# Output stores cut per batch entry, the last copy and its stores moved to other engines, the last gate cut in halves

## The chip, the cores and the metric

The kernel runs on one core of one Trainium2 chip. The metric is device time in microseconds (us) of one execution; the kernel before takes 823.6 us, the median of 3 runs (823.19 to 827.01). The core has a matrix engine (TensorE, PE in the rows; PEld is its weight load), three engines for elementwise work (VectorE or DVE, ScalarE or ACT, GpSimd or POOL), and a fifth, SyncE or SP, which here only issues DMA transfers. Each engine works through its own list of instructions in order and waits on semaphores for the others. A letter q behind a name (SPq) means the engine's sequencer, which issues transfers. The transfers of all of them are carried out by 16 DMA engines.

## The reference

A recurrence over 768 time steps, for 4 batch entries with 8 heads of 40, feeds a gated feed-forward layer:

```python
for t in range(S):                                   # S = 768
    y[:, :, t] = einsum('bhd,bhde->bhe', r_t, state)
    Sa = einsum('bhde,bhe->bhd', state, a_t)
    state = state * w_t[:, :, None, :] - Sa x b_t + v_t x k_t
x = y as (4 * 768, 320)                              # rows: batch entry, then time
h = x @ w_in                                         # 320 -> 2048
g = where(h >= 1, h, where(h <= -1, 0, (h + 1)**2 / 4))
out = g @ w_out                                      # 2048 -> 320, float32
```

## The kernel before

The recurrence runs in 24 chunks of 32 steps, each in two halves of 16 (batch, head) pairs. Lines 139 to 590 load and scale its rows, write them to scratch in DRAM (`scr`), read them back in another order (`ti`, `cg`, `tiab`), and do the chunk's small matrix products. Each 64 steps of finished rows make one of 12 groups: `relayout` (L605 to L614) moves the group's rows from `Y` into `X`, one of two buffers used in turn, with 6 transfers.

The feed-forward layer is the generator `moe`. A group holds 64 steps of 4 batch entries, 256 columns. For each of 8 expert pairs `k` (256 columns of the 2048 each):

- `first` (L631): 16 products of 256 columns into a PSUM bank `ph`, 8 for each half `j` of the pair; the two banks are used in turn.
- `gate`: Relu (L639) and Square (L640) on ScalarE, then minimum and maximum on VectorE (L642), each over the tile of 128 x 512, both halves at once.
- `split`: ScalarE rounds the result to `gh` (L648), GpSimd forms the rest `gl` (L649). Both tiles have one buffer.
- `second` (L661): 12 products of 320 columns with `gh` (8) and `gl` (4) into two PSUM banks `po`. Block 0 of the output (`po[0]`) holds batch entries 0 and 1 of the group's 64 steps, block 1 (`po[1]`) entries 2 and 3.

The loop is staggered: `first` of a pair stands ahead of `second` of the pair before it, and the gate of the new pair runs beside that. After the last pair's `first` and the `second` of the pair before, nothing is left to lay beside the last gate, split and `second`.

At a group's end ScalarE copies the two blocks to `ob` (L664). The stores go into a list, `deferred`; SP issues them (L666) at the next call of `catch_up`, in SP's list among the loads of the recurrence. So for each group SP issues 2 stores of 160 KB, each 128 partitions of `ob` to 2 x 64 rows of 1,280 bytes in `out`: the DRAM side is 2 batch entries, each a run of 64 rows.

The order of all this is written by hand: `feed` pulls so many columns of `moe` into each stage of the recurrence, `fill` and `background` put the preparation of later rows in between. When the recurrence is done, the rest of `moe` is emptied in one loop. `DMAHW0` to `DMAHW7` are 8 semaphores that the transfers of SP (and of ScalarE) use in turn; a transfer waits until the one 8 places ahead has landed.

Of the kernel before, what the change touches and what calls it, by code (L numbers as in the profile page):

```python
# [9 lines left out]
F32 = mybir.dt.float32  # L10
# [5 lines left out]
AF = mybir.ActivationFunctionType  # L16
ALU = mybir.AluOpType
# [3 lines left out]
NB, NHD, D, L = 4, 8, 40, 32  # L21
# [34 lines left out]
def rwkv_moe_kernel(ctx: ExitStack, tc: tile.TileContext, r, k, v, w, a, b, w_in, w_out, ident_d, mask_d, out):  # L56
    nc = tc.nc
# [5 lines left out]
    NF = FF // 128  # L63
# [6 lines left out]
    phs = [psa.tile([128, 512], F32, name=f"ph{i}") for i in range(2)]  # L70
    pos = [psa.tile([128, 512], F32, name=f"po{i}")[:, 0:320] for i in range(2)]
# [4 lines left out]
    half_c = const.tile([128, 1], F32, name="half_c")  # L76
# [6 lines left out]
    mp = ctx.enter_context(tc.tile_pool(name="mp", bufs=1))  # L83
# [13 lines left out]
    Y, Xt = [], {}  # L97
# [46 lines left out]
    flat = lambda x: x.rearrange("p a e -> p (a e)")  # L144
# [449 lines left out]
    groups = [(t, 64) for t in range(0, S, 64)]  # L594
# [23 lines left out]
    ov = out.rearrange("(b s) e -> b s e", b=NB)  # L618
    Xs = {}
    deferred = []  # L620

    def moe():

        def first(g, k):
            t0, nt = groups[g]
            n = NB * nt
            for j in range(2):
                f = 2 * k + j
                fs = slice(128 * (f % 4), 128 * (f % 4) + 128)
                for i, (xi, wi) in enumerate(MM1):  # L630
                    nc.tensor.matmul(  # L631
                        phs[k % 2][:, n * j : n * j + n], lhsT=wt[0, f // 4, wi // 2][:, wi % 2, fs], rhs=Xs[g][:, xi, :], start=i == 0, stop=i == 7
                    )
                    yield 15 * n // 16

        def gate(k):
            ph = phs[k % 2]
            gt = mp.tile([128, 512], F32, tag="gt", name="gt", bufs=2)
            nc.scalar.activation(gt, ph, AF.Relu, bias=half_c, scale=0.5)  # L639
            nc.scalar.activation(gt, gt, AF.Square)  # L640
            yield gt
            nc.vector.scalar_tensor_tensor(out=gt, in0=gt, scalar=1.0, in1=ph, op0=ALU.min, op1=ALU.max)  # L642
            yield

        def split(gt):
            gh = mp.tile([128, 512], F32R, tag="gh", name="gh", bufs=1)
            gl = mp.tile([128, 512], F32R, tag="gl", name="gl", bufs=1)
            nc.scalar.copy(gh, gt)  # L648
            nc.gpsimd.tensor_sub(gl, gt, gh.bitcast(F32))  # L649
            return gh, gl  # L650

        def second(g, k, gt, gh, gl):
            t0, nt = groups[g]
            n = NB * nt
            passes = [(x, i, j) for x, i in ((gh, 0), (gh, 1), (gl, 0)) for j in range(2)]
            for q, (x, i, j) in enumerate(passes):
                w = wt[1, 2 * k + j, 0][:, i, :]
                for i in range(n // 128):
                    ts_ = slice(n * j + 128 * i, n * j + 128 * i + 128)
                    end = q == 5 and k == NF // 2 - 1  # L660
                    nc.tensor.matmul(pos[i], lhsT=x[:, ts_], rhs=w, start=q == 0 and k == 0, stop=end)  # L661
                    if end:
                        ob = mp.tile([128, 320], F32, tag="ob", name="ob", bufs=2)
                        nc.scalar.copy(ob, pos[i])  # L664
                        m = 128 // nt
                        deferred.append(lambda ob=ob, i=i, m=m: nc.sync.dma_start(ov[m * i : m * i + m, t0 : t0 + nt, :], ob))  # L666
                    yield 320

        late = None
        for g in range(len(groups)):  # L670
            while g not in Xs:
                yield None
            for k in range(NF // 2):
                while g == 0 and converted[0] < needs(2 * k + 1):
                    next(wgen)
                if late:
                    late += split(late[2])
                yield from first(g, k)
                parts = gate(k)
                for i, d in enumerate(second(*late) if late else (320,) * 12):  # L680
                    yield d
                    if i == 3:
                        new = (g, k, next(parts))
                    elif i == 8:
                        next(parts)
                late = new
        yield from second(*late, *split(late[2]))

    jobs = []
    for j in range(4):  # L690
# [154 lines left out]
    i = 0  # L845
# [6 lines left out]
    adopt(0)  # L852
    Y.append(y_tile(F32R))
    mgen = moe()
    owed, idle = [0], [True]
    now = [0]
# [120 lines left out]
```

## Time and profile before

| | us |
|---|---|
| median of 3 runs (lowest, highest) | 823.6 (823.19, 827.01) |
| the profiled execution, its own time | 821.57 |
| its span, first to last instruction | 819.8 |
| TensorE busy | 679.4 |
| VectorE busy | 588.8 |
| ScalarE busy | 479.8 |
| GpSimd busy | 457.3 |

The span is what the trace shows; the profiled execution's own time is 1.77 us longer, and this execution lies 2.03 us below the median of the runs. The trace has the start and length of each instruction, what ended each wait, the share of the 16 DMA engines that were busy in any stretch, and the granted clock of TensorE there.

### The profile page before, as it was taken

What the parts mean: (1) busy time and instruction counts of PE and PEld (TensorE: products, weight loads), DVE (VectorE), ACT (ScalarE), POOL (GpSimd) and SP (SyncE); (2) the same over time, 40 slices, a digit from 0 to 9 for tenths busy, and PEclk for the clock granted to TensorE, in tenths of its full rate; (3) what the DMA queues carried; (4) which work ended last, traced back from release to release, by engine and by line L of the source; (5) the groups of instructions that cost most, each with busy time, mean ns of one, the idle gap of its engine ahead of it and who ended that gap; (6) DMA issues with size and microseconds to landing.
All of it is one profiled execution on the core that took longest, in us unless ns stands there. A gap on an engine that the chain in (4) does not pass through costs nothing.

```text
span 819.8 us, 35420 instructions
## 1 busy us (share of the span) xinstructions
PE 679.4 (83%) x15360; PEld 623.2 (76%) x15360; DVE 588.8 (72%) x1327; ACT 479.8 (59%) x1014; POOL 457.3 (56%) x630
## 2 busy tenths in 40 slices
PE   4265445598888688789988899999999999999994
PEld 4254445488777687679977789988899999999993
DVE  7996878778667567886767887767877777775220
ACT  5456666576564455656655566565665666665552
POOL 1305999965235869656648767554466742222331
PEclk9675556778899899999989999999999999999997
DMA  8888985756946636676436664352433324330100
GB/s 300 217 137 222 217 173 150 197 132 151 203 131 154 170 79 162 146 178 150 95 71 154 152 175 102 89 111 39 102 76 79 83 44 100 77 84 19 37 18 16
DMA packets 178714, 102.33 MB, mean 125 GB/s; under 512 B 123976, under 2 KB 171272, under 8 KB 178560
## 3 DMA queue, kind: packets, MB, share of 16 engines
q1 hardware_dynamic: 172288, 78.45, 42.5%
q0 software_dynamic: 6272, 21.63, 9.5%
q8 instruction: 121, 1.98, 1.0%
q14 instruction: 33, 0.27, 0.1%
HBM read 70.88 MB, written 27.53 MB: 120 GB/s over the span
## 4 chain that ended last, share of the span: by engine, by line
PE 49%; POOL 8%; DVE 5%; DMA 4%; ACT 3%; issue 2%; SPq 0%; ACTq 0%; POOLq 0%; DVEq 0%
PE po L661 16%; PE ph L631 16%; PE p L556 5%; PE p L545 3%; PE p L519 3%; DMA scr<-arena 2%; PE p L585 2%; POOL gl L649 2%; PE p L485 2%; POOL lw L369 2%; PE p L529 2%; POOL lw L363 2%; ACT gh L648 1%; DMA cg<-scr 1%; PE p L336 1%
## 5 line engine op out<-in xcount | busy, mean ns | idle before, releaser
L649 POOL TENSOR_TENSOR gl<-gt,gh 128x512 fp32r<-128x512 f32 x96 | 124.3, 1295 | 193.1 <-ACT gh L648 188.5
L631 PE MATMUL ph<-X,w 120*128 120x256 f32 x1536 | 217.3, 294 | 3.9 <-DMA X<-Y 3.6
L631 PEld LDWEIGHTS ph<-X,w 120*128 120x128 f32 x1536 | 196.0, 196 | 11.6 <-issue 4.8
L661 PE MATMUL po<-w,gh 128*128 128x320 f32 x768 | 135.9, 319 | 16.8 <-ACT gh L648 16.7
L661 PEld LDWEIGHTS po<-w,gh 128*128 128x128 f32 x768 | 117.1, 193 | 20.6 <-ACT gh L648 19.8
L642 DVE SCALAR_TENSOR_TENSOR gt<-gt,ph 128x512 f32<-128x512 f32 x96 | 65.8, 686 | 89.3 <-ACT gt L640 75.6
L639 ACT ACTIVATE gt<-ph,half_c 128x512 f32<-128x512 f32 x96 | 66.0, 687 | 54.7 <-PE ph L631 54.5
L563 DVE SCALAR_TENSOR_TENSOR cg<-p,pr 40x160 f32<-40x160 f32 x184 | 59.2, 322 | 53.1 <-PE p L556 51.1
L661 PE MATMUL po<-w,gl 128*128 128x320 f32 x384 | 78.0, 327 | 22.8 <-POOL gl L649 22.8
L369 POOL TENSOR_TENSOR lw<-lw 128x31 f32<-128x31 f32 (+15 forms) x155 | 88.2, 569 | 8.7
L363 POOL TENSOR_TENSOR lw<-lw 128x31 f32<-128x31 f32 (+15 forms) x155 | 85.8, 554 | 9.3
L661 PEld LDWEIGHTS po<-w,gl 128*128 128x128 f32 x384 | 63.0, 198 | 27.1 <-POOL gl L649 27.0
L497 DVE TENSOR_TENSOR cg<-p,mask 32x256 f32<-32x256 f32 x192 | 80.6, 420 | 3.5
L540 ACT ACTIVATE cg<-p 32x160 f32<-32x160 f32 x192 | 56.6, 295 | 26.8 <-PE p L529 12.0
L536 DVE SCALAR_TENSOR_TENSOR cg<-p,mask 32x128 f32<-32x128 f32 x192 | 55.2, 288 | 19.8 <-ACT cg L540 14.5
L550 ACT COPY ss<-p 40x320 f32<-40x320 f32 x92 | 38.6, 419 | 48.7 <-PE p L545 47.1
L556 PE MATMUL p<-cg 128*64 128x72 f32 (+1 forms) x1536 | 66.2, 246 | 0.0
L648 ACT CAST gh<-gt 128x512 fp32r<-128x512 f32 x96 | 59.7, 621 | 10.5 <-DVE gt L642 9.5
L640 ACT ACTIVATE gt<-gt 128x512 f32<-128x512 f32 x96 | 60.7, 632 | 3.1
L545 PE MATMUL p<-cg 128*40 128x40 f32 x1472 | 44.4, 224 | 21.8 <-ACT cg L540 15.4
L545 PEld LDWEIGHTS p<-cg 128*40 128x40 f32 x1472 | 38.1, 136 | 31.5 <-ACT cg L540 22.5
L556 PEld LDWEIGHTS p<-cg 128*64 128x64 f32 x1536 | 60.6, 155 | 0.4 <-issue 0.4
(100 smaller groups left out, 1100.0 us busy)
## 6 DMA issues: line engine op xcount, KB each, us to landing
ti<-scr SPq DMA_DIRECT2D x96, 200.0 KB
scr<-arena POOLq DMA_DIRECT2D x16, 640.0 KB, 5.8
cg<-scr SPq DMA_DIRECT2D x96, 80.0 KB
X<-Y SPq DMA_DIRECT2D x36, 160.0 KB
scr<-wide SPq DMA_DIRECT2D x8, 640.0 KB
w<-in_moe_w_out_dram POOLq DMA_DIRECT2D x16, 320.0 KB, 4.3
tiab<-scr SPq DMA_DIRECT2D x28, 160.0 KB
cg<-scr SPq DMA_DIRECT2D x96, 40.0 KB
```

The lines of the kernel that those rows point to most:

```text
L363: eng.tensor_mul(t3, W3[:, 0:n, j : j + 1].broadcast_to([128, n, m]), L3[:, j + 1 :, j].unsqueeze(1).broadcast_to([128, n, m]),)
L369: eng.tensor_sub(W3[:, 0:n, j + 1 :], W3[:, 0:n, j + 1 :], t3)
L497: nc.vector.tensor_tensor(out=cg[q, f::2, C_X : C_X + 64][:, 4 * i : 4 * i + 4].rearrange("p h (j x) -> p h j x", x=32), in0=ps[quarter(f, ...
L545: nc.tensor.matmul(pst[er[h % 2], h // 2, :], lhsT=cg[:, h, C_S : C_S + D], rhs=cg[:, h, C_G : C_G + D], start=True, stop=True)
L556: nc.tensor.matmul(psv[h // 8][64 * f : 64 * f + 64, h // 2 % 4, 0:n3], lhsT=cgw[:, h * CW + C_G : h * CW + C_G + 64], rhs=cg[:, h, C_R : ...
L631: nc.tensor.matmul(phs[k % 2][:, n * j : n * j + n], lhsT=wt[0, f // 4, wi // 2][:, wi % 2, fs], rhs=Xs[g][:, xi, :], start=i == 0, stop=i ...
L639: nc.scalar.activation(gt, ph, AF.Relu, bias=half_c, scale=0.5)
L640: nc.scalar.activation(gt, gt, AF.Square)
L642: nc.vector.scalar_tensor_tensor(out=gt, in0=gt, scalar=1.0, in1=ph, op0=ALU.min, op1=ALU.max)
L648: nc.scalar.copy(gh, gt)
L649: nc.gpsimd.tensor_sub(gl, gt, gh.bitcast(F32))
L661: nc.tensor.matmul(pos[i], lhsT=x[:, ts_], rhs=w, start=q == 0 and k == 0, stop=end)
```

## The change

- A new helper, `store`, issues one transfer for each batch entry: 64 partitions of `ob` to 64 consecutive rows of `out`, 80 KB. Each group has 4 stores where it had 2.
- Block 1 of the last group is copied by VectorE instead of ScalarE, and its 2 stores are issued by ScalarE. All other stores stay with SP.
- The last pair's gate is a function of its own, `last_gate`. It works on the halves `j` of 256 columns, in the order of the code below, and puts `gh` and `gl` in the buffer of `X` that the last group doesn't use. `second` of the pair ahead of it stands before it in the program. The last `second` takes both `gh` products of half 0 first, then those of half 1.

```diff
+    def store(ob, i, t0, nt, queue):
+        m = 128 // nt
+        for q in range(m):
+            queue.dma_start(ov[m * i + q, t0 : t0 + nt, :], ob[nt * q : nt * q + nt])
...
             passes = [(x, i, j) for x, i in ((gh, 0), (gh, 1), (gl, 0)) for j in range(2)]
+            if (g, k) == at_last:
+                passes = [(gh, i, j) for j in range(2) for i in range(2)] + passes[4:]
...
                         ob = mp.tile([128, 320], F32, tag="ob", name="ob", bufs=2)
-                        nc.scalar.copy(ob, pos[i])
-                        m = 128 // nt
-                        deferred.append(lambda ob=ob, i=i, m=m: nc.sync.dma_start(ov[m * i : m * i + m, t0 : t0 + nt, :], ob))
+                        at_end = g == len(groups) - 1 and i
+                        (nc.vector.tensor_copy if at_end else nc.scalar.copy)(ob, pos[i])
+                        deferred.append(lambda ob=ob, i=i, q=nc.scalar if at_end else nc.sync: store(ob, i, t0, nt, q))
...
+        def last_gate(k):
+            n = NB * groups[-1][1]
+            gt = mp.tile([128, 512], F32, tag="gt", name="gt", bufs=2)
+            spare = flat(Xt[len(groups) % 2])
+            gh, gl = (spare[:, 512 * i : 512 * i + 512] for i in range(2))
+            cols = [slice(n * j, n * j + n) for j in range(2)]
+            for x in cols:
+                nc.scalar.activation(gt[:, x], phs[k % 2][:, x], AF.Relu, bias=half_c, scale=0.5)
+                nc.scalar.activation(gt[:, x], gt[:, x], AF.Square)
+            for x in cols:
+                nc.vector.scalar_tensor_tensor(
+                    out=gt[:, x], in0=gt[:, x], scalar=1.0, in1=phs[k % 2][:, x], op0=ALU.min, op1=ALU.max
+                )
+            for x in cols:
+                nc.scalar.copy(gh[:, x], gt[:, x])
+                nc.gpsimd.tensor_sub(gl[:, x], gt[:, x], gh[:, x].bitcast(F32))
+            return gt, gh, gl
...
                 yield from first(g, k)
+                if (g, k) == at_last:
+                    yield from second(*late)
+                    late = g, k, *last_gate(k)
+                    break
                 parts = gate(k)
...
-        yield from second(*late, *split(late[2]))
+        yield from second(*late)
```

ScalarE's list at the end of the program, before, from the rounding of the pair ahead of the last (`ph_64` is the bank of the last pair, `po_65` and `po_66` are blocks 0 and 1; each row says on which semaphores the instruction waits):

```order
L648 CAST gh<-gt 128x512 [waits DVE_49,PE_49,Pool_49]
L639 ACTIVATE gt<-ph_64,half_c 128x512 [waits PE_49]
L640 ACTIVATE gt<-gt 128x512 [waits Activation_49]
L648 CAST gh<-gt 128x512 [waits DVE_49,PE_49,Pool_49]
L664 COPY ob<-po_65 128x320 [waits DMAHW6_49,PE_49]
L664 COPY ob<-po_66 128x320 [waits DMAHW7_49,PE_49]
```

The same piece of the changed program (`X_1896` is the spare buffer of `X`, where `gh` and `gl` now are):

```order
L654 CAST gh<-gt 128x512 [waits DVE_49,PE_49,Pool_49]
L685 ACTIVATE gt<-ph_64,half_c 128x256 [waits PE_49]
L686 ACTIVATE gt<-gt 128x256 [waits Activation_49]
L685 ACTIVATE gt<-ph_64,half_c 128x256
L686 ACTIVATE gt<-gt 128x256 [waits Activation_49]
L692 CAST X_1896<-gt 128x256 [waits DVE_49] x2
L673 COPY ob<-po_65 128x320 [waits DMAHW3_49,DMAHW2_49,PE_49]
L626 DMA out_dram<-ob 64x320 [waits DMAHW7_49,DVE_49]
L626 DMA out_dram<-ob 64x320 [waits DMAHW1_49]
```

Three instructions of 512 columns became six of 256, the second copy left the list, and two stores came into it. Only the first Relu waits for TensorE; the second waits for nothing.

SP's list at the first group's stores, before (`ld_...` and `scr` are loads and copies for later rows of the recurrence):

```order
L253 DMA ld_b<-in_b_dram 128x1x320
L253 DMA ld_w<-in_w_dram 128x1x320
L304 DMA tiab<-scr_107 32x16x80 x2
L666 DMA out_dram<-ob 2x64x320 x2
L253 DMA ld_a<-in_a_dram 128x1x320
L139 DMA scr_108<-in_v_dram 32x32x40
```

The same place of the changed program:

```order
L253 DMA ld_b<-in_b_dram 128x1x320
L253 DMA ld_w<-in_w_dram 128x1x320
L304 DMA tiab<-scr_107 32x16x80 x2
L626 DMA out_dram<-ob 64x320 x4
L253 DMA ld_a<-in_a_dram 128x1x320
L139 DMA scr_108<-in_v_dram 32x32x40
```

Two stores more stand ahead of the load of `ld_a`; nothing changes places. It is the same at the other groups, but the last, where SP keeps 2 stores of 64 rows and ScalarE has the other 2.

## Rows read from the trace of the kernel before

**Rows 1.** Waits of SP's queue, whole span: us in total, times, longest.

```profile
SPq L304 <- DVE ev L467: 159.0, 26, 13.6
...
SPq L973 <- DMA out_dram<-ob: 7.8, 2, 4.5
```

**Rows 2.** Stretches at the end: us, five engines' busy us, PEclk, DMA share, GB/s.

```profile
810.00:810.20 0.20, 0.00 (x0) 0.00 (x0) 0.00 (x0) 0.00 (x0) 0.00 (x0) 1.00 0.00 0
810.20:810.40 0.20, 0.00 (x0) 0.00 (x0) 0.00 (x0) 0.00 (x0) 0.00 (x0) 1.00 0.09 26
...
813.00:814.00 1.00, 0.00 (x0) 0.00 (x0) 0.00 (x0) 0.00 (x0) 0.00 (x0) 0.50 0.13 49
...
817.60:817.80 0.20, 0.00 (x0) 0.00 (x0) 0.00 (x0) 0.00 (x0) 0.00 (x0) 0.50 0.14 51
817.80:818.00 0.20, 0.00 (x0) 0.00 (x0) 0.00 (x0) 0.00 (x0) 0.00 (x0) 0.50 0.02 6
```

**Rows 3.** Timeline of the end: start, us, engine, line, operation [idle before, releaser].

```profile
803.72 0.69 ACT L639 ACTIVATE gt<-ph,half_c 128x512 f32<-128x512 f32 x1 [0.82 <-PE ph L631]
...
804.44 0.63 ACT L640 ACTIVATE gt<-gt 128x512 f32<-128x512 f32 x1
...
804.70 0.75 PE L661 MATMUL po<-w,gl 128*128 128x320 f32 x4
805.16 0.69 DVE L642 SCALAR_TENSOR_TENSOR gt<-gt,ph 128x512 f32<-128x512 f32 x1 [2.99 <-ACT gt L640]
805.96 0.62 ACT L648 CAST gh<-gt 128x512 fp32r<-128x512 f32 x1 [0.89 <-DVE gt L642]
...
806.63 1.44 PE L661 MATMUL po<-w,gh 128*128 128x320 f32 x8 [1.18 <-ACT gh L648]
...
808.73 0.75 ACT L664 COPY ob<-po 128x320 f32<-128x320 f32 x2 [2.16 <-PE po L661]
809.18 1.12 SPq L666 DMA_DIRECT2D out_dram<-ob  x2
```

**Rows 4.** Stretches after the stores at 595 us; loads of `ti`, `cg` start at 599.4.

```profile
599.00:600.00 1.00, 1.00 (x9) 1.00 (x8) 0.34 (x1) 0.76 (x2) 0.92 (x3) 1.00 0.13 49
...
601.00:602.00 1.00, 1.00 (x57) 0.96 (x59) 0.62 (x2) 0.90 (x3) 0.86 (x2) 1.00 1.00 304
```

**Rows 5.** Groups by line and form, whole span: busy us, mean ns | idle before.

```profile
L497 DVE TENSOR_TENSOR cg<-p,mask 32x256 f32<-32x256 f32 x192 | 80.6, 420 | 3.5
...
L576 POOL TENSOR_TENSOR Y<-yt,Y 128x256 fp32r<-128x256 f32 x48 | 36.4, 759 | 32.2 <-ACT Y L575 29.6 <-DMA cg<-scr 2.5
...
L575 ACT CAST Y<-yt 128x256 fp32r<-128x256 f32 x48 | 19.4, 404 | 1.0
...
L175 DVE TENSOR_TENSOR wide<-wide 128x320 f32<-128x320 f32 x6 | 3.0, 492 | 0.2
```

**Rows 6.** SP's issues of `ti` and `scr`: ns min/median/max of one issue.

```profile
L304 SPq DMA_DIRECT2D ti<-scr x96: 302/441/1547, 22.8 to 721.8; - x96
...
L225 SPq DMA_DIRECT2D scr<-wide x8: 616/730/2435, 17.6 to 70.4; - x8
```

**Rows 7.** Timeline after the first group's stores, columns as in Rows 3.

```profile
228.51 1.34 SPq L666 DMA_DIRECT2D out_dram<-ob  x2
...
229.96 0.60 SPq L253 DMA_DIRECT2D ld_a<-in_a_dram  x1
...
234.00 0.92 POOL L290 DMA_DIRECT2D scr<-arena  x1 [0.30 <-POOL arena L289]
...
241.36 0.77 ACT L272 COPY arena<-ld_w 128x320 f32<-128x320 f32 x1 [4.05 <-DMA scr<-arena]
```

**Rows 8.** The page's transfers: count, KB each, median us from issue to landing.

```profile
scr<-arena POOLq DMA_DIRECT2D x16, 640.0 KB, 5.8
```

**Rows 9.** SP's timeline at the stores of a later group.

```profile
643.80 1.25 SPq L666 DMA_DIRECT2D out_dram<-ob  x2
648.17 0.80 SPq L304 DMA_DIRECT2D ti<-scr  x2
```

More of the change, by code (lines that the diff above doesn't have):

```diff
@@ L663, in second @@
                         ob = mp.tile([128, 320], F32, tag="ob", name="ob", bufs=2)
-                        nc.scalar.copy(ob, pos[i])
-                        m = 128 // nt
-                        deferred.append(lambda ob=ob, i=i, m=m: nc.sync.dma_start(ov[m * i : m * i + m, t0 : t0 + nt, :], ob))
+                        at_end = g == len(groups) - 1 and i
+                        (nc.vector.tensor_copy if at_end else nc.scalar.copy)(ob, pos[i])
+                        deferred.append(lambda ob=ob, i=i, q=nc.scalar if at_end else nc.sync: store(ob, i, t0, nt, q))
                     yield 320
+        def last_gate(k):
[15 more added lines that the diff above has]
+            return gt, gh, gl
         late = None
+        at_last = len(groups) - 1, NF // 2 - 1
         for g in range(len(groups)):
```

## The prediction

> **What bounds the kernel now.** The shares of busy time come first and say little: TensorE works 679.4 of 819.8 us, but no engine's total tells what happens after the last product. So I went to the waits of SP's queue, which closes the program. There the reader sees that SP ends by waiting 7.8 us for the last stores [rows 1], with nothing else left to do. The table of stretches shows the same from the side of the DMA engines: the last data flows from 810.2 to just past 817.8 us, with every compute engine at 0.00, at 49 to 51 GB/s and a DMA share of 0.13 to 0.14 [rows 2]. The share is over 16 engines, so it is 2 of them, each moving about 25 GB/s. The two stores, 327,680 bytes together, share the same two engines: 327,680 bytes at 49 to 51 GB/s would take 6.4 to 6.7 us, and the start is slower. The shape explains the 2: the DRAM side of a store is 2 x 64 x 320.
>
> Third, the timeline of the end [rows 3]. The last pair's `first` ends at 803.70; Relu, Square, minimum and maximum, rounding follow one another to 806.58; TensorE has finished the pair before at 804.70 + 0.75 = 805.45 and stands idle until 806.63 (1.18 us). The first copy starts at 808.73, SP issues from 809.18 to 810.30. So the stretch that the change touches is the 16.1 us from 803.70 to 819.8, half of it two DMA engines' work.
>
> **The stores at the end.** Removed are 2 transfers of 128 packets of 1,280 bytes; added are 4 of 64. With 2 engines, 256 packets are 128 each; from 810.2 to 817.85 that is 7.65 / 128 = 60 ns a packet. Nothing in the trace of before stores 64 rows to one run of DRAM. The nearest rows are the loads of `ti` and `cg`, whose outer count is 32: with them the share goes from 0.13 to 1.00, 304 GB/s [rows 4]. So a transfer of 32 outer rows uses all 16 engines, and I take 16 for 64. Each engine then has 4 packets per store, 0.24 us; even all four stores at once are 16 packets, 0.96 us. The other end is that nothing changes, 7.65 us.
>
> The Trainium skill (DMA: Bandwidth & Descriptors, "Why a DMA increments its semaphore by 16 and not by 1") has the number of engines as the largest number up to 16 that divides the slowest dimension of both sides. By it 128 against 2 gives 2, and the trace's 0.13 agrees; 64 against 64 gives 16, which no run here shows yet; the span would be 812.8 at the end by it, where rows alone leave it between 812.8 and 819.4 (the 6.6 us of the two engines kept). The same page ("Rules for kernel authors") speaks against the change: two transfers of partition halves are said not to be worth it, since both spread over the same engines, and one of 128 partitions should be used. By that rule the end would stay where it is (the first rival); the 0.13 of one such 128-partition store says that its condition, spreading over all engines, doesn't hold here.
>
> **The last copy and the issues.** Before, the second copy ends at 809.48 and SP issues twice, 0.56 us each, the second from about 809.75. After, VectorE copies block 1 beside ScalarE: 0.49 us by an operation of 128x320 [rows 5]. Each of the two queues issues twice. An issue costs 0.30 to 0.44 us for 32 outer rows, at worst 2.4 [rows 6]; I take 0.56. ScalarE has issued no transfer before, so its first is unknown from 0.30 to 2.4 us; I take 0.56 for it too. Nothing is queued behind ScalarE's waiting stores.
>
> **The last gate by halves.** It looks like an early start for half 0, 8 products before half 1 is done. It isn't: in ScalarE's list the first Relu waits for TensorE and the second for nothing, though it reads half 1; so the first must already wait for all 16 products. The gate starts at 803.72 as before. What is left is shorter links. Half lengths: rounding 0.62 to 0.404 (128x256 [rows 5]), that is 0.217 less; Relu 0.69 to 0.47 and Square 0.63 to 0.415 by the same difference; VectorE 0.42 (256 columns), GpSimd 0.76. With the gaps of [rows 3]:
> ScalarE's four end at 804.19, 804.64, 805.14, 805.58. VectorE's half 0 should start after the first Square; I let it start only after the second Relu, at 805.22 (the second Relu is what the program seems to signal; starting at 804.72 is no use to ScalarE, which is busy to 805.58, and gives 0.1 us), to 805.65; half 1 to 806.09. Rounding to 806.15 and 806.59. TensorE starts at 806.20 instead of 806.63, four products of 0.168 to 806.87, four more to 807.54 (rounded half 1 ready at 806.64). GpSimd ends at 806.98 and 807.77; the `gl` products run from 807.54 and 807.88 without a wait. Gain 0.43, with ends 0 (GpSimd's halves as slow as wholes) and 1.36 (TensorE never idle). The spare buffer of `X` takes away the wait for `gl`'s readers, which end at 805.45 and bind nobody here.
>
> **The sum of the end.** Copy 0 at 808.73 - 0.43 = 808.30; SP's store at 808.75. Copy 1 on VectorE from 808.45 to 808.95; ScalarE issues at 808.98 and 809.55. Data came 1.04 us after the start of the issue before (809.18 to 810.22), so the last data starts at 810.6 and ends at 810.85. From the last data to the end of the span it was 819.8 - 817.85 = 1.95; I keep it: 812.8. That is 7.0 us less, 6.8 of it by the shorter transfer.
>
> **The other eleven groups.** SP gets 2 more issues each, 2 x 0.56 = 1.1 us. In seven of these places SP then waits anyway, as from 645.05 to 648.17 [rows 9], 3.1 us, mostly for `ev` [rows 1]; after two there is nothing to load soon. Only in two does a load follow at once, as `ld_a` at 229.96 [rows 7]. If both delays reached the path whole, they would cost 2.3 us. On the other side, two engines no longer have 7 us of store ahead of whatever comes next. At 234.00 GpSimd's 640 KB transfer lands 7.28 us after its issue (just before ScalarE's 241.36, which waited 4.05 for it), against a median of 5.8 [rows 7, 8]: 1.5 us to win. I take 1.0 gained; bounds 2.3 lost, 4 gained (the same at two or three crowded places).
>
> Together 8.0: span 811.8, own time 813.6 with the 1.77 outside it. The median of the runs before lies 2.03 above the profiled execution; I forecast for that median: 823.6 - 8.0 = 815.6.
>
> **Rivals.**
> - *The store stays on two engines, or its end is bound by something else than packets.* Only gate, copy and issues are left: about 0.7 us, 822.9. For it: no row shows a 64-row store. Against: rows 4. 4%.
> - *SP becomes late.* The longer issue reaches the loads of the recurrence in ten groups: 10 x 1.12 = 11.2 us lost against 7.0 gained, 4.2 us more than before, 827.8, slower. It decides from the point where SP's waits behind the stores are under 1.1 us; they are 3 us and more in seven places. 3%.
> - *The recurrence gains more.* With the two crowded engines free, transfers on the chain land earlier in several places: 4 us instead of 1.0, 812.6, or less. The trace names the transfer at 234 only. 10%.
> - *ScalarE's first issue is slow*, 2.4 us, and the recurrence gains nothing: 815.6 + 1.9 + 1.0 = 818.5. 8%.
>
> My forecast itself has 75%; its own range is 813.5 to 817.5. The range for 8 in 10 runs from 812.5 to 818.5. About 0.5% (4.1 us) is what a measurement of this kernel can tell from no change: faster than 819.5 has 0.92 (all but the first two rivals and a small remainder), slower than 827.7 has 0.03 (the second rival), the same 0.05.
>
> **What would show it.** In the profile after: a DMA share near 1, not 0.13, in the stretch after the last issue, for less than 1 us; SP's last wait for `out_dram` 1 to 2 us instead of 7.8; the first half Relu at the end of all 16 products; TensorE idle 0.75 us before the last products instead of 1.18; the first arena wait shorter than 4.05. The prediction is wrong if the share stays at 0.13, if the time from last data to the end grows, or if the recurrence's part of the span moves by more than 3 us.

## The result, and the profile after

The changed kernel takes 817.31 us (median of 12 runs, 812.82 to 820.73) where the kernel before takes 823.91 (12 runs on the same chip, 818.38 to 827.6): a ratio of 0.9917, with a 95% interval of 0.9889 to 0.9946. Two later measurements of the same code gave 0.9871 [0.9836, 0.9907] and 0.9871 [0.9824, 0.9918] (e10, e13 below). The forecast was 815.6, with a range of 812.5 to 818.5. Throughout, ratios leave out executions in a slower state (four of the kernel before beside e1 to e4, 829.89 to 834.22, and one of e13, 820.43), medians have them all, and a ratio differs from the quotient of the two medians by up to 0.0022.

The profiled execution took 816.67 us, its span is 814.8. Its end, in the timeline (start, us, engine, line, operation, [idle before, releaser]):

```profile
803.36 2.08 PE L637 MATMUL ph<-X,w 120*128 120x256 f32 x16
...
805.47 0.47 ACT L685 ACTIVATE gt<-ph,half_c 128x256 f32<-128x256 f32 x1 [0.82 <-PE ph L637]
805.98 0.42 ACT L686 ACTIVATE gt<-gt 128x256 f32<-128x256 f32 x1
806.30 0.46 ACT L685 ACTIVATE gt<-ph,half_c 128x256 f32<-128x256 f32 x1
...
806.45 0.75 PE L669 MATMUL po<-w,gl 128*128 128x320 f32 x4
...
806.87 0.80 DVE L688 SCALAR_TENSOR_TENSOR gt<-gt,ph 128x256 f32<-128x256 f32 x2 [2.94 <-ACT gt L685]
807.32 0.79 ACT L692 CAST X<-gt 128x256 fp32r<-128x256 f32 x2
...
807.77 2.07 PE L669 MATMUL po<-w,X 128*128 128x320 f32 x12 [0.57 <-ACT X L692]
...
809.74 0.43 ACT L673 COPY ob<-po 128x320 f32<-128x320 f32 x1 [1.63 <-PE po L669]
809.89 0.49 DVE L673 COPY ob<-po 128x320 f32<-128x320 f32 x1 [2.22 <-PE po L669]
810.19 1.11 SPq L626 DMA_DIRECT2D out_dram<-ob  x2
810.41 1.18 ACTq L626 DMA_DIRECT2D out_dram<-ob  x2
```

Call F the end of the last pair's 16 products: 803.70 before, 805.45 here. F itself moves by several microseconds between executions of one kernel (804.42 to 808.47 in three of the changed kernel), so the end is measured from F. Before, F to the first copy is 5.03 us and F to the end of the span 16.1 [rows 3]; here 4.29 and 9.35. That is 6.75 us less: 0.74 in the gate and the last products, 6.0 after the first copy.

What became of the stores stands in the stretches of one microsecond at the end (us, five engines' busy us, PEclk, DMA share, GB/s):

```profile
811.00:812.00 1.00, 0.00 (x0) 0.00 (x0) 0.00 (x0) 0.00 (x0) 0.00 (x0) 1.00 0.61 142
812.00:813.00 1.00, 0.00 (x0) 0.00 (x0) 0.00 (x0) 0.00 (x0) 0.00 (x0) 1.00 0.69 186
```

and in stretches of 0.2 us:

```profile
811.40:811.60 0.20, 0.00 (x0) 0.00 (x0) 0.00 (x0) 0.00 (x0) 0.00 (x0) 1.00 0.98 224
...
812.00:812.20 0.20, 0.00 (x0) 0.00 (x0) 0.00 (x0) 0.00 (x0) 0.00 (x0) 1.00 1.02 275
...
812.80:813.00 0.20, 0.00 (x0) 0.00 (x0) 0.00 (x0) 0.00 (x0) 0.00 (x0) 1.00 0.03 6
```

A share of 0.13 to 0.14 for 7.65 us [rows 2] has become one of 0.61 and 0.69 in two stretches, near 1 inside them (0.98, 1.02), and the data ends at about 812.8. SP's waits (us in total, times, longest) say the same:

```profile
SPq L1005 <- DMA out_dram<-ob: 1.8, 2, 1.5
```

The closing wait for `out_dram` is 1.8 us where it was 7.8 [rows 1].

### The profile page after: what moved, and what is told of

It is laid out like the page before. It is cut to its first block, busy times and chain, and to the rows that moved or that the text cites. A ratio compares the mean times of both kernels' runs of the same rounds, so it can differ in the third digit from the quotient of the medians.

```text
span 814.8 us, 35447 instructions
## 1 busy us (share of the span) xinstructions
PE 677.7 (83%) x15360; PEld 621.9 (76%) x15360; DVE 588.3 (72%) x1329; ACT 479.8 (59%) x1016; POOL 456.0 (56%) x631
## 4 chain that ended last, share of the span: by engine, by line
PE 52%; POOL 5%; DVE 5%; ACT 4%; DMA 4%; issue 2%; SPq 0%; POOLq 0%; ACTq 0%; DVEq 0%
PE ph L637 17%; PE po L669 16%; PE p L556 5%; PE p L545 3%; DMA scr<-arena 3%; PE p L519 3%; PE p L585 2%; PE p L485 2%; PE p L529 2%; POOL gl L655 1%; POOL lw L363 1%; POOL lw L369 1%; PE p L336 1%; ACT gh L654 1%; DVE cg L587 1%
## 5 line engine op out<-in xcount | busy, mean ns | idle before, releaser
L669 PE MATMUL po<-w,gh 128*128 128x320 f32 x760 | 134.1, 319 | 15.9 <-ACT gh L654 15.9
```

## The experiments

Three questions were open: which of the edits the end owes its 6.75 us to, why the first half Relu waits for all 16 products, and whether the smaller stores of the other eleven groups do anything to the recurrence. For the last, one theory has the two crowded DMA engines delay the transfers behind a store (old stores cost, new ones gain); its rival has SP's two extra issues for each group cost time, and a third says that neither matters. All kernels below are edits of the changed kernel, most of them a single one (e2 and e9 have several). The table has what all of them showed; the time is against the kernel before on the same chip, and a run without a ratio was executed once.

| kernel | F | F to first copy | F to end | ratio [95%] | median us (before) |
|---|---|---|---|---|---|
| before | 803.70 | 5.03 | 16.1 | | |
| changed | 805.45 | 4.29 | 9.35 | 0.9917 [0.9889, 0.9946] | 817.31 (823.91) |
| e1, old stores inside | 806.17 | 4.29 | 9.23 | 0.9946 [0.9919, 0.9974] | 819.40 (825.26) |
| e2, stores only | 810.60 | 5.05 | 11.0 | 0.9960 [0.9931, 0.9988] | 820.97 (825.26) |
| e3, old stores everywhere | 808.65 | 4.30 | 15.75 | 1.0003 [0.9972, 1.0034] | 826.38 (825.26) |
| e4, no stores inside | 810.36 | 4.30 | 9.24 | 0.9894 [0.9863, 0.9925] | 816.21 (825.26) |
| e6, 62 + 2 rows at the end | 811.10 | 4.31 | 15.4 | one run | 828.33 (827.36) |
| e7, 61 + 3 rows inside | 835.40 | 4.30 | 9.2 | 1.0171 [1.0136, 1.0206] | 842.57 (827.36) |
| e8, SP issues all | 803.14 | 4.29 | 10.26 | one run | 815.23 (826.36) |
| e9, two banks | 808.00 | 3.28 | 8.3 | 0.9887 [0.9856, 0.9917] | 817.25 (827.36) |
| e10, changed again | 804.42 | 4.30 | 9.38 | 0.9871 [0.9836, 0.9907] | 814.89 (827.36) |
| e11, 32 + 32 rows inside | 804.60 | 4.29 | 9.2 | 0.9903 [0.9871, 0.9936] | 817.57 (826.36) |
| e12, old stores inside again | 803.70 | 4.28 | 9.3 | 0.9921 [0.9891, 0.9951] | 820.12 (826.36) |
| e13, changed, third time | 808.47 | 4.29 | 9.33 | 0.9871 [0.9824, 0.9918] | 817.02 (826.36) |

**e1: the old stores in the first eleven groups.** The end keeps all of the change.

```diff
+        if t0 != groups[-1][0]:
+            queue.dma_start(ov[m * i : m * i + m, t0 : t0 + nt, :], ob)
+            return
         for q in range(m):
```

> The change as it stands, but the first eleven groups are stored as before, by 2 transfers of 2 x 64 rows; only the last group has 4 transfers of 64 rows. Theory A (the gain is made at the end of the program): same as the changed kernel, about 6.6 us below the kernel before, and 9.35 us from the last product of the last first to the end of the span, as there (805.45 to 814.8). Theory B (part of the gain comes from the eleven groups inside the recurrence, whose loads no longer stand behind two busy DMA engines): 1 to 4 us slower than the changed kernel, with the same 9.35 us at the end. Under both, the arena transfer after the first group's stores waits as long as before (ScalarE 4.05 us).

The end is 9.23 us and the time 0.9946: the last group's edits alone bring most of the gain. What the other groups' stores add is too small to be read from this one ratio, whose interval overlaps that of the changed kernel. ScalarE's wait for GpSimd's transfer after the first group's stores is 4.36 us, as long as before (4.05 [rows 7]).

**e2: only the stores.** Gate, order of the last products, copy and issuing queue are as before.

```diff
-            if (g, k) == at_last:
-                passes = [(gh, i, j) for j in range(2) for i in range(2)] + passes[4:]
...
-                        at_end = g == len(groups) - 1 and i
+                        at_end = False
...
-                if (g, k) == at_last:
-                    yield from second(*late)
-                    late = g, k, *last_gate(k)
-                    break
...
-        yield from second(*late)
+        yield from second(*late, *split(late[2]))
```

> Only the stores are cut per batch entry; gate, order of products and both last copies as before, all 4 last stores issued by SP. Worked out from the two traces: the first copy at 5.03 us after the last product of the last first (before), the four issues at 0.55 us each from 5.48, the last from 7.13, and 3.82 us from its start to the end of the span (changed kernel): 10.95 us, against 16.1 before and 9.35 with the whole change. Theory A: 5.2 us below the kernel before (ratio 0.9937). A rival, that the gate and the two engines make most of the gain, would leave it within 2 us of the kernel before.

Its timeline at the end:

```profile
808.52 2.08 PE L637 MATMUL ph<-X,w 120*128 120x256 f32 x16
...
815.65 0.75 ACT L671 COPY ob<-po 128x320 f32<-128x320 f32 x2 [2.16 <-PE po L667]
816.10 2.38 SPq L626 DMA_DIRECT2D out_dram<-ob  x4
```

The end is 11.0 us (810.60 to 821.6): 5.1 of the 6.75 come from the shape of the stores alone. Put on top of it, the gate gives 0.75 and copy and queue 0.9.

**e3: the rest without the stores.** One transfer of 2 x 64 rows for each block, in all groups.

```diff
-        for q in range(m):
-            queue.dma_start(ov[m * i + q, t0 : t0 + nt, :], ob[nt * q : nt * q + nt])
+        queue.dma_start(ov[m * i : m * i + m, t0 : t0 + nt, :], ob)
```

> The other half alone: gate by halves, last copy by VectorE, last store issued by ScalarE, but all stores are one transfer of 2 x 64 rows per block, as before. Theory A: the DMA share at the end is 0.13 again for 7 to 8 us, the end takes 15.2 to 15.4 us instead of 16.1, time 0.7 to 0.9 us below the kernel before (no measurable change). Rival (a second issuing queue brings its own DMA engines): share 0.25, the end about 12 us.

Two queues issue here, 0.22 us apart, and the stores still move on two engines; the stretches of e3 (columns as above):

```profile
817.00:818.00 1.00, 0.00 (x0) 0.00 (x0) 0.00 (x0) 0.00 (x0) 0.00 (x0) 0.50 0.13 29
820.00:821.00 1.00, 0.00 (x0) 0.00 (x0) 0.00 (x0) 0.00 (x0) 0.00 (x0) 0.50 0.13 49
```

The share is again 0.13 and the ratio cannot be told from 1. A second issuing queue brings no DMA engines. The end is 15.75 us, where 15.2 to 15.4 was expected: the gate gives its 0.73, but from the first copy to the end it is 11.45 us against 11.07 before, so with the old stores copy and queue cost 0.4 instead of giving 0.9. ScalarE's one issue takes 1.14 us there, SP's 0.51; why the end is later isn't shown. The gains therefore don't add: 5.1 (e2) and 0.35 (e3) by themselves, 6.75 together.

**e8: SP issues all four last stores**, executed once.

```diff
-                        deferred.append(lambda ob=ob, i=i, q=nc.scalar if at_end else nc.sync: store(ob, i, t0, nt, q))
+                        deferred.append(lambda ob=ob, i=i, q=nc.sync: store(ob, i, t0, nt, q))
```

> The changed kernel with all four last stores issued by SP; VectorE still makes the second copy. SP's issues start 0.45 us after the first copy and take 0.55 us each, the last starts 2.1 us after the first copy instead of ScalarE's 1.25, so the end is 0.8 us later: 10.2 us from the last product of the last first to the end of the span, against 9.35. Rival (ScalarE's first issue costs as much as it saves): 9.4.

Its timeline at the end:

```profile
807.43 0.42 ACT L673 COPY ob<-po 128x320 f32<-128x320 f32 x1 [1.63 <-PE po L669]
807.58 0.49 DVE L673 COPY ob<-po 128x320 f32<-128x320 f32 x1 [2.22 <-PE po L669]
807.88 2.38 SPq L626 DMA_DIRECT2D out_dram<-ob  x4
```

Four issues in a row take SP 2.38 us and the end is 10.26, 0.9 more than with two queues. From the first copy to the end it is 5.97 us, and 5.95 in e2 where ScalarE makes both copies. So VectorE's copy is worth nothing while SP issues alone, and the 0.9 comes with the second queue. Whether that queue needs the copy beside it to begin early isn't shown, since no run has it without.

**e6: the last group's stores cut into 62 and 2 rows**, executed once. Nearly the same transfers as in the changed kernel, with another divisor.

```diff
+        cuts = (0, 62, 64) if t0 == groups[-1][0] else (0, 64)
+        for c, d in zip(cuts, cuts[1:]):
+            for q in range(m):
+                queue.dma_start(ov[m * i + q, t0 + c : t0 + d, :], ob[nt * q + c : nt * q + d])
```

> In the last group each batch entry's store of 64 rows is cut into one of 62 rows and one of 2. The Trainium skill (DMA: Bandwidth & Descriptors, the section on why a DMA increments its semaphore by 16) has the number of DMA engines as the largest number up to 16 that divides the outer count: 2 for 62 rows. Theory A (that rule): the DMA share at the end falls back to 0.13, and from the last issue to the end of the data it takes 7 us and more, so about 15 us from the last product of the last first to the end of the span instead of 9.35. Rival (64 rows are fast because they are one run of rows on the DRAM side, spread over all engines whatever their number): share 0.6 to 1, the end 10 to 11.5 us with four more issues.

A stretch of e6, and SP's last wait:

```profile
822.00:823.00 1.00, 0.00 (x0) 0.00 (x0) 0.00 (x0) 0.00 (x0) 0.00 (x0) 0.50 0.14 50
```

```profile
SPq L1007 <- DMA out_dram<-ob: 7.2, 2, 5.9
```

Two engines again, 50 GB/s, and an end of 15.4 us. Two rows fewer cost 6 us: what counts is by what the number of rows can be divided, not whether a store lies in one run of DRAM or covers half the partitions.

**e9: half 1 of the last pair in a PSUM bank of its own**; besides, the last four of the 12 products of `second`, those with `gl`, are sorted by block, so that block 0 is done earlier, and each block's two last stores go to SP and ScalarE, one each.

```diff
+        def half(g, k, j):
+            n = NB * groups[g][1]
+            if j and (g, k) == at_last:
+                if not spare:
+                    spare[0] = psum()
+                return spare[0][:, n : 2 * n]
+            return phs[k % 2][:, n * j : n * j + n]
...
-            for x in cols:
-                nc.scalar.activation(gt[:, x], phs[k % 2][:, x], AF.Relu, ...)
+            for j, x in enumerate(cols):
+                nc.scalar.activation(gt[:, x], half(g, k, j), AF.Relu, ...)
...
+            if (g, k) == at_last:
+                steps = steps[:8] + steps[8::2] + steps[9::2]
...
-            queue.dma_start(ov[m * i + q, t0 : t0 + nt, :], ob[nt * q : nt * q + nt])
+            (nc.scalar if q and t0 == groups[-1][0] else nc.sync).dma_start(
+                ov[m * i + q, t0 : t0 + nt, :], ob[nt * q : nt * q + nt])
```

> The changed kernel, with half 1 of the last pair's first in a PSUM bank of its own, the last products with gl ordered block 0 before block 1, and SP and ScalarE each issuing one store per block. Theory A of the gate (the first half Relu waits for all 16 products because both halves lie in one bank): with two banks it starts right behind the pair before, 0.8 us before the last product of first; TensorE isn't idle before the last products; the first copy 3.5 us after the last product of first (4.29 in the changed kernel), last issue from 4.5, end of the span 8.3 to 8.5 us after it (9.35). Rival (the order of the instructions in the program makes the wait): no change at the gate, 9.0. Time: 0.9 us below the changed kernel, not measurable by time alone.

Its timeline (`p` is the bank of half 1):

```profile
805.93 1.12 PE L648 MATMUL ph<-X,w 120*128 120x256 f32 x8
...
806.88 1.12 PE L648 MATMUL p<-X,w 120*128 120x256 f32 x8
807.13 0.47 ACT L699 ACTIVATE gt<-ph,half_c 128x256 f32<-128x256 f32 x1
...
807.62 0.42 ACT L700 ACTIVATE gt<-gt 128x256 f32<-128x256 f32 x1
...
808.15 0.42 DVE L702 SCALAR_TENSOR_TENSOR gt<-gt,ph 128x256 f32<-128x256 f32 x1 [1.66 <-ACT gt L700]
...
809.02 0.75 PE L683 MATMUL po<-w,gl 128*128 128x320 f32 x4
...
809.61 1.92 PE L683 MATMUL po<-w,X 128*128 128x320 f32 x12
811.28 0.42 ACT L687 COPY ob<-po 128x320 f32<-128x320 f32 x1 [1.42 <-PE po L683]
```

The first half Relu starts 0.87 us before the last of the 16 products ends, TensorE goes from the pair before to the last products without a stop, and the end is 8.3 us, 1.05 less than in the changed kernel; 1.01 of it lies ahead of the first copy (3.28 against 4.29), so the queues gave nothing. How the 1.01 is shared between bank and order of products isn't separated. The wait itself belongs to the shared bank: the first half Relu starts before the reordered products come, and the order of ScalarE's instructions is the same here. VectorE shows it too: its half 0 starts 0.11 us after the first Square (808.04), while it started 0.11 after the second Relu in the changed kernel (806.87, Relu until 806.76). The new bank is also a new tile; but here VectorE reads half 0 of `gt`, one tile as well though not in PSUM, while ScalarE is still writing half 1 (808.04 to 808.52), so one tile by itself doesn't make such a wait. The end is the shortest of all. Its time, 0.9887 [0.9856, 0.9917], cannot be told from that of the changed kernel on the same chip (e10).

**e4: no stores in the first eleven groups.** Their rows of the output are left out.

```diff
+        if t0 != groups[-1][0]:
+            return
         for q in range(m):
```

> The changed kernel without any store of the first eleven groups (their rows of the output are left out); the last group as in the change. Takes away the whole cost that stores have inside the recurrence. Theory A: same as the changed kernel, within 1.5 us. Theory B (the extra issues of SP and the transfers still hold up the recurrence): 2 to 5 us faster than the changed kernel.

0.9894: a kernel that stores nothing inside is as fast as the changed one within the intervals (0.9871 to 0.9917). So inside the recurrence stores of 64 rows cost no more than these intervals allow, about 3 us.

**e7: 61 and 3 rows in the first eleven groups**, which puts nearly the whole store on one engine, against **e11: 32 and 32 rows**, with as many issues (8 for each group).

```diff
+        cuts = (0, 61, 64) if t0 != groups[-1][0] else (0, 64)      # e7
+        cuts = (0, 32, 64) if t0 != groups[-1][0] else (0, 64)      # e11
+        for c, d in zip(cuts, cuts[1:]):
+            for q in range(m):
+                queue.dma_start(ov[m * i + q, t0 + c : t0 + d, :], ob[nt * q + c : nt * q + d])
```

> In the first eleven groups each store of 64 rows is cut into 61 and 3 rows; the last group as in the change. By the same rule 61 rows go to one DMA engine: 4 x 61 packets of 60 ns behind one another, 14.6 us per group instead of 7.65 on two engines (before) and 1 us on 16 (the change), and 4 more issues per group. Doubles what theory B holds responsible. Theory A (the recurrence doesn't feel the stores): within 1.5 us of the changed kernel run beside it. Theory B (the loads behind the busy engines are on the path): 3 to 10 us slower than the changed kernel run beside it.

> In the first eleven groups each store of 64 rows is cut into two of 32: 8 issues per group, as many as in the run with 61 and 3 rows, but 32 divides by 16, so every transfer uses all 16 DMA engines. Tells apart what made that run 15 us slower than the kernel before: theory A (the one busy engine, and what stands behind it) expects this one within 2 us of the changed kernel beside it; theory B (four more issues of SP per group, 2.2 us each, and their places among the 8 semaphores) expects 10 to 22 us more.

e7 takes 842.57 us, 1.0171 of before; e11 0.9903. That is 27.7 us above the changed kernel on e7's chip (e10, 814.89), well beyond both expectations of e7 (within 1.5, or 3 to 10). The number of issues is the same, so the 22 us between the two ratios (0.0268 of 827) are not SP's issues as such. The waits of e7:

```profile
ACT tiab L310 <- DMA tiab<-scr: 29.2, 12, 5.8
...
POOL arena L273 <- DMA ld_a<-in_a_dram: 10.6, 1, 10.6
```

```profile
SPq L445 <- DMA out_dram<-ob: 14.8, 6, 2.8
```

Loads that come behind the stores land late (`tiab` 29.2 us of waits, 7.5 in the changed kernel), and SP waits for its own stores before it reuses their semaphores (the changed kernel has no such wait before its end). Its list at the first group's stores, in e7 and then in e11:

```profile
227.73 9.70 SPq L628 DMA_DIRECT2D out_dram<-ob  x8
237.54 0.94 SPq L253 DMA_DIRECT2D ld_a<-in_a_dram  x1
```

```profile
228.32 4.15 SPq L628 DMA_DIRECT2D out_dram<-ob  x8
232.57 0.55 SPq L253 DMA_DIRECT2D ld_a<-in_a_dram  x1
```

Behind the stores of e7 the DMA share is that of a single engine of 16 for several us:

```profile
231.00:232.00 1.00, 1.00 (x38) 0.90 (x37) 0.97 (x3) 0.60 (x3) 0.70 (x1) 1.00 0.07 24
```

Eight issues take 9.70 us there and 4.15 here. Crowding of an engine reaches the recurrence in two ways, by late loads and by issues that get longer. The rival that issues by themselves cost 10 to 22 us falls: e11 has twice as many as the changed kernel, and its interval overlaps all three of that kernel's.

**e10 and e13: the changed kernel again; e12: e1 again.** They ask whether two engines, as before the change, cost the recurrence anything.

> The changed kernel itself, for comparison with the others on this chip: 9.35 us from the last product of the last first to the end of the span, 6.6 us below the kernel before.

> The changed kernel beside the two above: 6.75 us below the kernel before if the gain is that of the end alone; 8 to 10 if the recurrence gains as well.

> The run with the old stores in the first eleven groups once more, beside the changed kernel on one chip. Its end is that of the changed kernel (9.2 to 9.4 us after the last product of the last first), its recurrence that of the kernel before. If the recurrence doesn't feel two busy engines: within 1 us of the changed kernel; if it does: 2 to 4 us slower.

e12 and e13 ran on one chip: 0.9921 and 0.9871, with intervals that overlap. By medians e12 is 3.1 us slower, as expected if the recurrence feels the old stores (2 to 4), and e13 gains 9.3, in the 8 to 10 expected if it gains too; neither is clear of the noise. The profiles differ behind the first group's stores, the place that the forecast named. SP's list there, in e12 (2 stores of 2 x 64 rows) and in e13 (4 of 64):

```profile
226.40 1.37 SPq L626 DMA_DIRECT2D out_dram<-ob  x2
227.87 0.60 SPq L253 DMA_DIRECT2D ld_a<-in_a_dram  x1
228.53 1.63 SPq L139 DMA_DIRECT2D scr<-in_v_dram  x1
231.62 1.69 SPq L253 DMA_DIRECT2D ld_k<-in_k_dram  x1
231.89 0.92 POOL L290 DMA_DIRECT2D scr<-arena  x1 [0.30 <-POOL arena L289]
233.35 0.60 SPq L139 DMA_DIRECT2D scr<-in_r_dram  x1
...
239.53 0.78 ACT L272 COPY arena<-ld_w 128x320 f32<-128x320 f32 x1 [4.32 <-DMA scr<-arena]
```

```profile
227.19 2.51 SPq L626 DMA_DIRECT2D out_dram<-ob  x4
229.79 0.97 SPq L253 DMA_DIRECT2D ld_a<-in_a_dram  x1
230.81 0.62 SPq L139 DMA_DIRECT2D scr<-in_v_dram  x1
232.41 0.57 SPq L253 DMA_DIRECT2D ld_k<-in_k_dram  x1
232.68 0.92 POOL L290 DMA_DIRECT2D scr<-arena  x1 [0.30 <-POOL arena L289]
233.04 0.59 SPq L139 DMA_DIRECT2D scr<-in_r_dram  x1
...
238.99 0.80 ACT L272 COPY arena<-ld_w 128x320 f32<-128x320 f32 x1 [3.00 <-DMA scr<-arena]
```

Behind the two large stores two later issues take 1.63 and 1.69 us instead of 0.62 and 0.57, so SP needs 7.55 us from the first store to the end of the last load with the old stores (226.40 to 233.95) and 6.44 with the new (227.19 to 233.63), two issues more included. This stretch of SP's list repeats: 7.44 to 7.56 us in the four executions with old stores inside (before, e1, e3, e12), 6.43 to 6.47 in the six with four stores of 64 rows (changed, e2, e8, e9, e10, e13). The four issues alone vary, from 2.51 us in e13 to 3.74 in e10, against 1.34 to 1.37 for the two old ones. GpSimd's 640 KB from 231.89 release ScalarE 7.64 us later in e12, and 6.31 in e13 from 232.68. Over the executions profiled, this time is 7.36 to 7.66 in the four with old stores inside (before [rows 7], e1, e3, e12) and 5.11 to 6.60 in the seven with stores of 64 rows or none (changed, e2, e4, e8, e9, e10, e13); e11 with its 32 rows lies between, at 7.14. So SP's list wins about 1.1 us at this place and GpSimd's transfer 1.3 on average (7.55 against 6.23). That either reaches the end of the program isn't shown.

## Why the prediction was right, step by step

**The bound and the store.** Right. The stores of 64 rows move on all 16 engines, and this is 5.1 of the 6.75 us (e2). The forecast gave the shorter transfer 6.8 of its 7.0, and 0.7 to gate, copy and issues in its first rival; that split was wrong, as e2 and e3 show (5.1 and 0.35 alone, 1.3 only where both are there). The Trainium skill (DMA: Bandwidth & Descriptors, "Why a DMA increments its semaphore by 16 and not by 1") is borne out by 62 rows as well: the largest number up to 16 that divides 62 is 2, and e6 shows a share of 0.13 to 0.14. The Trainium skill's advice on the same page against two transfers of partition halves ("Rules for kernel authors") does not hold for this store: it rests on the whole transfer using all 16 engines, and this one used 2; halving it brought the 5.1 us.

A size was off: the sum has the data of one last store take 0.24 us and the last of it done 2.55 us after the first copy's start; it was 3.06 (809.74 to about 812.8). A packet cost more than the 60 ns taken: each engine had 16, and the shares of 0.61 and 0.69 make 1.30 us of them, 81 ns each. So the share is near 1 for about 1.5 us (811.2 to 812.8, with a slow start and end), and not for less than 1 as was named. That two queues send at once isn't the reason: in e8, where SP alone issues, the shares sum to 1.37 us, 86 ns each. From the last data to the end it is 2.0 us, as kept (1.95). Hence 6.0 us after the first copy where the forecast had 6.57.

**The last copy and the issues.** Right in sum. ScalarE's first issue, unknown before, is like any other (times, ns min/median/max of one issue):

```profile
L626 ACTq DMA_DIRECT2D out_dram<-ob x2: 542/571/600, 810.4 to 811.0; - x2
```

It took 542 to 600 ns against the 560 taken, and the rival of a slow first issue falls for this store (the one of e3, with 2 x 64 rows, took 1.14 us). What the text did not see is that the copy has no worth of its own while SP issues alone (e8).

**The last gate by halves.** The mechanism was right: the first half Relu starts at F + 0.02, with half 1 done. e9 shows its cause, the shared bank, which the forecast had only from ScalarE's list. The term was mis-sized: 0.74 instead of 0.43. The second Relu starts 0.10 before the Square ends (806.30 against 806.40), VectorE's halves take 0.40 and TensorE is idle 0.57 us, not 0.75: it starts at F + 2.32 where F + 2.50 was worked out. From there to the first copy it is 1.97 us, and was 2.10 before.

**The end together.** 6.75 where 7.0 was forecast: the gate gave 0.31 more and what follows the first copy 0.57 less, so two errors in part cancel.

**The other eleven groups.** 1.0 gained was forecast, between 2.3 lost and 4 gained. The mechanism, two crowded engines ahead of GpSimd's 640 KB, is there at the place named, with 1.1 to 1.3 us in place of the 1.5 to win; ScalarE's wait there is 3.22 us where it was 4.05 [rows 7]. The two more issues took SP 2.0 us there instead of 1.1 (four take 3.38, two took 1.34), but this was won back, since the issues behind the old stores were themselves longer. For the whole, subtract each kernel's gain at the end (16.1 less its F to end) from its gain in time (the ratio on the median before). What is left, in us, with intervals of about 2.3 to 3.9 either way:

| stores inside | time gained beyond the end |
|---|---|
| 64 rows, 32 rows or none: changed, e10, e13, e9, e11, e4, e2 | 0.1, 4.0, 3.9, 1.5, 1.1, 1.9, -1.8 |
| 2 x 64 rows: e1, e12, e3 | -2.4, -0.3, -0.6 |

The means are 1.5 and -1.1, so 2.6 us apart in favour of the new stores, but the rows overlap (e2, with new stores, has -1.8). Beside one another on one chip, and with equal ends, e1 lies 3.2 us above e4, which stores nothing inside, and e12 3.1 above e13 (medians); by an estimate from the scatter of these runs, the first is known to about 2.3 us and the second to about 4.6 either way. So the old stores cost the recurrence something against no stores at all; against stores of 64 rows it is likely and not shown. The profiles can't settle it: F itself lay between 804.42 and 808.47 in three executions of the changed kernel. The forecast's 1.0 fits, and 4 is not excluded. What is shown is 1.1 to 1.3 us at one place, and that the effect grows to about 22 us when one engine gets the store (e7 against e11); how much two engines cost in all stays open.

**The total.** 8.0 us were forecast; by the ratios it is 6.8 in the first measurement and 10.7 in e10 and in e13. The 6.75 at the end repeats within 0.03 us (F to end 9.35, 9.38, 9.33). That the first median, 817.31, lies 1.7 us from the forecast's 815.6 owes something to luck: what the recurrence adds, forecast at 1.0, came out as 0.1 there and as 4.0 and 3.9 in the other two.

**The rivals.** The store on two engines: refuted (e6 and e3 show what it would have looked like, ends of 15.4 and 15.75). SP becoming late: refuted by e11, with twice the issues. The recurrence gaining 4 us: not shown, not excluded. A slow first issue: refuted.

## What to carry to other kernels

Read the DMA share in the stretch where only a transfer runs: 0.13 means two engines of 16, and then look at the number of rows on the DRAM side before looking at bytes or queues. Cut a transfer so that its outermost count on both sides has 16 as a divisor; 64 rows do, 2 x 64, 62 and 61 don't (shares near 1, then 0.13, 0.13 and 0.07). In this program the reader of half a PSUM bank waited for the writer of the other half, and started 0.87 us before that writer's end once the halves had a bank each (e9): for overlap by halves, give them two banks.

## What the runs showed of the hardware

- An engine's packet of 1,280 bytes took 60 ns when 2 engines worked, and about 81 ns when 16 did (1.30 us for 16 packets; in e12 0.33 + 0.93 + 0.03 of three stretches, 1.29 us; 86 ns in e8, with one queue).
- Issues slow down behind a store that few engines carry: eight issues on SP took 9.70 us with nearly all of the data on one engine (e7) and 4.15 with 32 rows each (e11); behind stores on two engines one load's issue took 1.63 us instead of 0.62 (e12, e13).
- About 2 us pass between the last data of a store and the end of the program, with either shape of store (1.95 and 2.0).
